# Strassen's products in the last two token tiles of a sparse-attention and feed-forward kernel

## The chip, the cores and the metric

The kernel runs on one core of one Trainium2 chip. The metric is the device time of one execution in microseconds (us), and the figure of a kernel is the median over its executions. The engines are TensorE (PE; its weight loads are PEld), VectorE (DVE), ScalarE (ACT), GpSimd (POOL) and SyncE (SP, which issues the transfers).

## The reference

Eight batches with eight heads of 576 tokens and 64 elements pass through a sparse causal attention: four heads see a local window of 32 tokens, four see every 32nd token. The result, 4608 tokens by 512, goes through a feed-forward layer without a nonlinearity other than a product.

```python
scores = scale * np.matmul(q, k.transpose(0, 1, 3, 2))      # masked, softmax
x = attn_out.transpose(0, 2, 1, 3).reshape(B * S, H * D)    # 4608 x 512
a = x @ w1                                                  # w1, w2: 512 x 1024
b = x @ w2
h = a * b @ w3                                              # w3: 1024 x 1024
return h @ w_out                                            # 1024 x 512
```

## The kernel before

The attention output is kept transposed in fp16, in four tiles `xT[0]` to `xT[3]` of 128 features by 4608 tokens. `xT[hp]` holds head pair `hp`; pairs 0 and 1 are the local heads, 2 and 3 the strided ones. `w3 @ w_out` is formed once on the chip into `w34`, so that the feed-forward layer is three matmuls for each tile of 512 tokens: there are nine such tiles (0 to 8).

For a tile and a block `jc` of 128 of the 1024 d_ff columns, `a` (L956) sums four matmuls of 128x512 into one PSUM bank, one for each `xT`. ACT copies it to SBUF (`asb`, L309). `b` (L972) sums four more into another bank, and DVE multiplies both into `abt` in fp16 (L978, "mul"). After eight blocks four output groups `o` of 128 tokens follow (L992), eight matmuls each. ACT copies each to `osb` and SP stores it. The groups are written as `o6_2` for tile 6, group 2, and `a7_0` for tile 7, block 0.

The attention of batch b runs between the matmuls of tile b-1. For each head pair it has a score group on PE (`S7_3` is batch 7, pair 3; L794), an exponential on ACT (L811), a mask on DVE (L818), a value group on PE in two halves (`X7_3_0` and `X7_3_1`) and a normalisation. For pairs 2 and 3 that is `ln` and `rcp` on ACT (L874, L885) for each half and then two multiplications on DVE into `xT` (L901), called "norm" here. Pairs 0 and 1 are normalised on DVE and transposed back by PE. Pair 3 of a batch is last.

PSUM has four single banks (kind "f": `a`, `b`, `o`, transposes) and two pairs (kind "B": scores and values). Inputs are loaded as fp32 into eight staging tiles `st0` to `st7` of 128x1024 and cast by POOL.

Every piece of work is an `Op` with engine, estimated duration, dependencies, buffers taken and given back, and a rank. `Plan.order` (L89) walks through time and gives each free engine the ready operation with the lowest rank. The result is one fixed order for each engine; at run time each engine works through its order and waits at semaphores. The ranks of tile t lie at 100 + 24 t, and those of the attention come from `_arank`:

```python
base = {0: 40, 1: 60}.get(b, 100 + 24 * (b - 1) - 4)
a = plan.op(f"a{t}_{jc}", {"PE": 864}, fa, ..., rank=100 + 24 * t + 2 * jc + 1)
h = plan.op(f"o{t}_{ts}_{pt}_{hf}", ..., rank=100 + 24 * t + 17 + 2 * ts + 0.001 * hf)
```

Of the kernel before, what the change touches and what calls it, by code (L numbers as in the profile page):

```python
# [16 lines left out]


def _arank(b, i, ph):
    base = {0: 40, 1: 60}.get(b, 100 + 24 * (b - 1) - 4)  # L20
    span = {0: 4, 1: 12}.get(b, 24)
    return base + span * (i / 4 + OFF[ph])


def _loads():
# [6 lines left out]
    for b in range(2, 8):  # L32
# [6 lines left out]

CFG = dict(loads=_loads(), arank=_arank, frank=lambda j: 50 + j, slack=100,  # L40
           pord=lambda b: (2, 3, 0, 1) if b < 2 else (0, 1, 2, 3), tsplit=False, dmaf=1.08, nhr=8, cast=dict(w1=dict(POOL=1040)),
           first=('DVE', 'ACT', 'POOL'), early=0, pm=4, nx=4, nstg=8, new=(2, 3), lb=3, ll=4, nat={'POOL': 1160})


def _ap(t: bass.AP, off_add, dims):
# [215 lines left out]
def kernel(  # L261
# [12 lines left out]
    cfg = CFG  # L274
# [24 lines left out]
    NSTG = cfg.get("nstg", 8)  # L299
    NABT = cfg.get("nabt", 3)  # L300
    stgs = [consts.tile([P, DF], FP32, name=f"st{i}") for i in range(NSTG)]
    plan = Plan(dict(f=NF, B=2, stg=NSTG, asb=2, osb=3, rcp=2, xqs=2, xqd=cfg.get("nxq", 2), w3n=3, abt=NABT))

    def pin(ins):
        return tc.keep_in_program_order(ins)
# [383 lines left out]
    for b in range(B):  # L689
# [30 lines left out]
        for pi, hp in enumerate(cfg["pord"](b)):  # L720
# [78 lines left out]
            for g in range(2):  # L799
# [31 lines left out]
                                                 ptms[pslot][0:kr, h * 288 + i * w:h * 288 + (i + 1) * w],  # L831
                                                 start=True, stop=True))

                def fpo(e, b=b, hp=hp, g=g, pk=pk, w=w, m=m, kr=kr, local=local, pslot=pslot):
                    xps = bank("B", pk, [P, 2, 512], FP32)
                    vt = (v16L if local else v16S)[b % 2]
                    for i in range(m):
                        for h in range(2):
                            c0 = h * 288 + i * w
                            pin(nc.tensor.matmul(xps[0:w, h, i * 65:(i + 1) * 65], ptms[pslot][0:kr, c0:c0 + w],  # L840
                                                 vt[0:kr, 2 * (hp % 2) + h, g * m + i, 0:D + 1],
                                                 start=True, stop=True))

                if old:
                    fp = fpo
                pv = PVop[(b, hp, g)] = plan.op(pk, {"PE": 246}, fp, deps=[mo, onesop[(b % 2, local)]] + vop[(b, hp, g)],
                                                take=[("B", pk)], rank=rank(f"P{g}"), soft=True)
                ptmu[pslot] = pv
                newPV[g] = pv

                if old:
                    def fn(e, pk=pk, w=w, m=m, g=g, xk=xk):
                        xps = bank("B", pk)
                        rcp = att.tile([P, 2, 4], FP32, tag="rcq", name="rcq")
                        if not xk:
                            xqs = att.tile([P, 4, 2, D], FP16, tag="xqs", bufs=2, name="xqs")
                            live[("xqs", pk)] = xqs
                        elif g == 0:
                            live[xk] = att.tile([LQ, LT, 2, D], FP16, tag="xqd", bufs=cfg.get("nxq", 2), name="xqd")
                        if xk:  # L860
                            xqs = live[xk][:, g * m:g * m + m]
                        xv = xps[0:w, :, 0:m * 65].rearrange("p h (i e) -> p h i e", e=65)
                        pin(nc.vector.reciprocal(out=rcp[0:w, :, 0:m], in_=xv[:, :, :, D]))
                        pin(nc.vector.tensor_mul(xqs[0:w, 0:m].rearrange("p i h d -> p h i d"), xv[:, :, :, 0:D],  # L864
                                                 _ap(rcp, 0, [[rcp.ap[0][0], w], [4, 2], [1, m], [0, D]])))

                    norms.append(plan.op(f"norm{nm2}_{g}", {"DVE": 190 + 60 + (554 if local else 690)}, fn,
                                         deps=[pv] + norms, take=[] if xk and g else [xk or ("xqs", pk)], give=[("B", pk)], rank=1))
                    continue


# [65 lines left out]
                                     deps=[t2, wf], give=[("f", tk)], rank=1)]  # L937


    for t in range(NTILE):  # L940
        tok = bass.ds(t * NT, NT)
        bs = range(t * NT // S, (t * NT + NT - 1) // S + 1)
        xd = [x for b in bs for h in range(4) for x in xTop[(b, h)]]
        muls = []

        def fz(e, t=t):
            big[("abt", t)] = ffn.tile([P, KF, NT], FP16, tag="abt", bufs=NABT, name="abt")

        z = plan.op(f"abt{t}", {"PE": 0}, fz, deps=xd, take=[("abt", f"abt{t}")], rank=100 + 24 * t - 20)
        for jc in range(KF):  # L950
            js = bass.ds(jc * P, P)

            def fa(e, jc=jc, t=t, js=js, tok=tok):
                ps = bank("f", f"a{t}_{jc}", [P, NT], FP32)
                for ci in range(KM):
                    pin(nc.tensor.matmul(ps, w1h[:, ci, js], xT[ci][:, tok], start=(ci == 0), stop=(ci == KM - 1)))  # L956

            a = plan.op(f"a{t}_{jc}", {"PE": 864}, fa, deps=[z] + w1c[jc], take=[("f", f"a{t}_{jc}")],
                        rank=100 + 24 * t + 2 * jc + 1)

            def fs(e, jc=jc, t=t):
                asb = ffn.tile([P, NT], FP32, tag="asb", bufs=2, name="asb")
                live[("asb", t, jc)] = asb
                copy(e, asb, bank("f", f"a{t}_{jc}"))

            s = plan.op(f"asb{t}_{jc}", cfg.get("asb", {"ACT": 590}), fs, deps=[a], take=[("asb", f"{t}_{jc}")],
                        give=[("f", f"a{t}_{jc}")], rank=4)

            def fb(e, jc=jc, t=t, js=js, tok=tok):
                ps = bank("f", f"b{t}_{jc}", [P, NT], FP32)  # L970
                for ci in range(KM):
                    pin(nc.tensor.matmul(ps, w2h[:, ci, js], xT[ci][:, tok], start=(ci == 0), stop=(ci == KM - 1)))  # L972

            bb = plan.op(f"b{t}_{jc}", {"PE": 864}, fb, deps=xd + w2c[jc] + [a], take=[("f", f"b{t}_{jc}")],
                         rank=100 + 24 * t + 2 * jc + 1.001)

            def fu(e, jc=jc, t=t):
                pin(nc.vector.tensor_mul(big[("abt", t)][:, jc, :], bank("f", f"b{t}_{jc}"), live[("asb", t, jc)]))  # L978

            muls.append(plan.op(f"mul{t}_{jc}", {"DVE": 690}, fu, deps=[bb, s],  # L980
                                give=[("f", f"b{t}_{jc}"), ("asb", f"{t}_{jc}")], rank=4))
        for ts in range(NT // P):
            last = t == NTILE - 1 and ts == NT // P - 1
            parts = ((0, 256), (256, 128), (384, 128)) if last else ((0, DM),)
            for pt, (n0, nw) in enumerate(parts):
                key = f"o{t}_{ts}_{pt}"
                h = None
                for hf in range(2):
                    def fo(e, t=t, ts=ts, hf=hf, key=key, n0=n0, nw=nw):
                        ps = bank("f", key, [P, nw], FP32) if hf == 0 else bank("f", key)  # L990
                        for ci in range(4 * hf, 4 * hf + 4):
                            pin(nc.tensor.matmul(ps, big[("abt", t)][:, ci, bass.ds(ts * P, P)],  # L992
                                                 w34[:, ci, bass.ds(n0, nw)], start=(ci == 0),
                                                 stop=(ci == KF - 1)))

                    h = plan.op(f"o{t}_{ts}_{pt}_{hf}", {"PE": 864 * nw // DM}, fo,
                                deps=[muls[4 * hf + i] for i in range(4)] + w34op[8 * hf:8 * hf + 8] + [h],
                                take=[("f", key)] if hf == 0 else [], rank=100 + 24 * t + 17 + 2 * ts + 0.001 * hf,
                                give=[("abt", f"abt{t}")] if ts == 3 and hf == 1 and pt == len(parts) - 1 else [])

                ok = "asb" if pt else "osb"

                def fc(e, key=key, nw=nw, ok=ok):
                    osb = ffn.tile([P, nw], FP32, tag=ok, bufs=3 if ok == "osb" else 2, name="osb")
                    live[("osb", key)] = osb
                    copy(e, osb, bank("f", key))

                oe = {"ACT": 170 + 4 * nw // 5, "DVE": 70 + 6 * nw // 5} if last else cfg.get("osb", {"ACT": 590})
                c = plan.op(f"osb{key}", oe, fc, deps=[h], take=[(ok, key)], give=[("f", key)], rank=4)

                def fd(e, key=key, t=t, ts=ts, n0=n0, nw=nw):
                    eng = nc.scalar if e == "ACT" else nc.sync
                    pin(eng.dma_start(out_r[t * (NT // P) + ts][:, bass.ds(n0, nw)], live[("osb", key)]))

                plan.op(f"st{key}", cfg.get("st", {"SP": 450}), fd, deps=[c],
                        give=[(ok, key)], rank=4.5, dma=750 * nw // DM, store=True)
# [42 lines left out]
```

## Time and profile before

| what | before |
|---|---|
| median of 13 runs | 272.5 us (271.52 to 274.1) |
| the profiled execution, its span | 271.57 us, 269.8 us |
| PE busy, matmuls | 259.4 us (96%), 2265 |
| DVE busy, ACT busy, POOL busy | 168.9 us, 156.1 us, 146.4 us |
| bytes moved by transfers | 54.41 MB, 202 GB/s |
| granted TensorE clock | 0.997 |

The page comes from one execution. Busy time is given as a share of the span; PE's is modelled, since matmuls overlap in the array, and a matmul of 512 columns is listed with 379 ns although the next one starts about 216 ns later. The 40 slices show when an engine works, and the chain of waits shows which work was last in line before the end. A group's idle time is that of its engine just before it, with the work that ended it.

### The profile page before, as it was taken

What the parts mean: (1) busy time and instruction counts of PE and PEld (TensorE: products, weight loads), DVE (VectorE), ACT (ScalarE), POOL (GpSimd) and SP (SyncE); (2) the same over time, 40 slices, a digit from 0 to 9 for tenths busy, and PEclk for the clock granted to TensorE, in tenths of its full rate; (3) what the DMA queues carried; (4) which work ended last, traced back from release to release, by engine and by line L of the source; (5) the groups of instructions that cost most, each with busy time, mean ns of one, the idle gap of its engine ahead of it and who ended that gap; (6) DMA issues with size and microseconds to landing.
All of it is one profiled execution on the core that took longest, in us unless ns stands there. A gap on an engine that the chain in (4) does not pass through costs nothing.

```text
span 269.8 us, 6083 instructions
## 1 busy us (share of the span) xinstructions
PE 259.4 (96%) x2265; PEld 141.5 (52%) x2265; DVE 168.9 (63%) x324; ACT 156.1 (58%) x280; POOL 146.4 (54%) x172
## 2 busy tenths in 40 slices
PE   7887899999999999999999999999999999999994
PEld 2466786545565545544544555455545554444443
DVE  6645566885787758766884787487659762422321
ACT  2870467764677764775577647756764774333331
POOL 6676997689879447964793389626980000000000
PEclk9999999999999999999999999999999999999998
DMA  7999999999699899899989998999995013003004
GB/s 242 348 359 272 348 356 351 307 272 315 210 258 231 147 269 206 192 202 278 209 203 188 266 165 201 177 278 197 191 206 146 0 41 117 2 22 135 0 4 155
DMA packets 72766, 54.41 MB, mean 202 GB/s; under 512 B 44256, under 2 KB 62048, under 8 KB 72736
## 3 DMA queue, kind: packets, MB, share of 16 engines
q1 hardware_dynamic: 72736, 54.02, 82.4%
q8 instruction: 18, 0.29, 0.5%
q14 instruction: 12, 0.10, 0.1%
HBM read 38.93 MB, written 9.44 MB: 179 GB/s over the span
## 4 chain that ended last, share of the span: by engine, by line
PE 87%; DMA 7%; SPq 2%; POOL 1%; issue 1%; DVE 1%; ACT 0%; POOLq 0%
PE ps_o L992 23%; PE ps_b L972 23%; PE ps_a L956 23%; DMA st<-in_moe_w_dram 7%; PE ps_S L794 4%; PE ps_mm L669 3%; PE ps_X L840 3%; PE ps_X L830 3%; PE ps_U L921 2%; SPq L316 2%; PE ps_T L747 1%; POOL w3n L313 1%; PE ps_tr L649 1%; PE ps_S L784 0%; PE ps_R L695 0%
## 5 line engine op out<-in xcount | busy, mean ns | idle before, releaser
L972 PE MATMUL ps_b<-xT,w2h 128*128 128x512 f16 x288 | 73.8, 379 | 0.2 <-DVE kTL L311 0.2
L956 PE MATMUL ps_a<-xT,w1h 128*128 128x512 f16 x288 | 73.9, 379 | 0.0
L978 DVE TENSOR_TENSOR abt<-ps_b,asb 128x512 f16<-128x512 f32 x72 | 49.7, 690 | 38.3 <-PE ps_b L972 35.1
L309 ACT COPY asb<-ps_a 128x512 f32<-128x512 f32 x72 | 42.1, 587 | 49.2 <-PE ps_a L956 48.9
L992 PE MATMUL ps_o<-w,abt 128*128 128x512 f16 (+2 forms) x304 | 67.3, 368 | 0.0
L313 POOL CAST xs<-st 80x1024 f16<-80x1024 f32 (+1 forms) x36 | 33.2, 941 | 19.3 <-DMA st<-in_q_dram 17.0
L972 PEld LDWEIGHTS <-w2h 128*128 128x128 f16 x288 | 26.7, 98 | 28.6 <-POOL w2h L313 0.7
L992 PEld LDWEIGHTS <-abt 128*128 128x128 f16 x304 | 27.2, 98 | 27.5
L956 PEld LDWEIGHTS <-w1h 128*128 128x128 f16 x288 | 26.5, 98 | 27.5
L811 ACT ACTIVATE ps_S<-ps_S 128x576 f32<-128x576 f32 (+2 forms) x56 | 32.8, 627 | 12.1 <-PE ps_S L794 12.1
L309 ACT COPY osb<-ps_o 128x512 f32<-128x512 f32 (+1 forms) x36 | 20.8, 578 | 24.1 <-PE ps_o L992 21.0
L901 DVE TENSOR_TENSOR xT<-ps_X,rcp 64x288 f16<-64x288 f32 x56 | 25.2, 450 | 13.6 <-ACT rcp L885 12.8
L313 POOL CAST v16L<-st 32x768 f16<-32x768 f32 (+1 forms) x32 | 26.3, 821 | 6.5 <-DMA st<-in_v_dram 4.9
L818 DVE TENSOR_TENSOR ptm<-ps_S,maskL 128x576 f16<-128x576 f32 x28 | 19.8, 750 | 9.4 <-ACT ps_S L811 9.3
L864 DVE TENSOR_TENSOR xqs<-ps_X,rcq 96x384 f16<-96x384 f32 (+1 forms) x36 | 20.5, 568 | 1.2
L313 POOL CAST v16S<-st 72x1024 f16<-72x1024 f32 (+1 forms) x16 | 16.5, 1037 | 5.6 <-DMA st<-in_v_dram 5.6
L885 ACT ACTIVATE rcp<-ps_X 64x576 f32<-64x576 f32 x28 | 18.1, 647 | 0.9
L874 ACT ACTIVATE ps_X<-ps_X 64x576 f32<-64x576 f32 x28 | 17.7, 631 | 0.3
L669 PE MATMUL ps_mm<-woh,xT 128*128 128x256 f16 x128 | 16.0, 273 | 1.6 <-POOL woh L313 1.6
L840 PEld LDWEIGHTS <-ptm 128*96 128x96 f16 (+1 forms) x224 | 14.5, 123 | 5.5 <-issue 0.2
L313 POOL CAST x<-st 128x1024 f16<-128x1024 f32 x14 | 14.4, 1039 | 4.7 <-DMA st<-in_q_dram 2.7
L311 DVE COPY xT<-ps_U 128x576 f16<-128x576 f16 x18 | 8.8, 490 | 11.3 <-PE ps_U L921 11.3
(82 smaller groups left out, 265.7 us busy)
## 6 DMA issues: line engine op xcount, KB each, us to landing
out_dram<-osb SPq DMA_DIRECT2D x35, 256.0 KB
st<-in_moe_w_dram SPq DMA_DIRECT2D x16, 512.0 KB
st<-in_v_dram SPq DMA_DIRECT2D x16, 288.0 KB
st<-in_v_dram SPq DMA_DIRECT2D x16, 256.0 KB
st<-in_q_dram SPq DMA_DIRECT2D x7, 512.0 KB
st<-in_k_dram SPq DMA_DIRECT2D x7, 512.0 KB
st<-in_q_dram SPq DMA_DIRECT2D x10, 256.0 KB
st<-in_k_dram SPq DMA_DIRECT2D x10, 256.0 KB
```

Of the source, the lines that this page charges most:

```text
L309: pin(nc.scalar.copy(out=out, in_=in_))
L313: pin(nc.gpsimd.tensor_copy(out=out, in_=in_))
L669: pin(nc.tensor.matmul(ps, w3T(kc)[:, js], big["woh"][:, kc, ns], start=(kc == 0), stop=(kc == KF - 1)))
L811: pin(nc.scalar.activation(out=sps, in_=sps, func=AF.Exp, bias=0.0, scale=scale))
L818: pin(nc.vector.tensor_mul(ptm[0:kr, 0:576].rearrange("p (h a x) -> p h a x", h=2, x=w), pte[0:kr].rearrange("p h (a x) -> p h a x", x=w), ...
L840: pin(nc.tensor.matmul(xps[0:w, h, i * 65:(i + 1) * 65], ptms[pslot][0:kr, c0:c0 + w], vt[0:kr, 2 * (hp % 2) + h, g * m + i, 0:D + 1], sta ...
L864: pin(nc.vector.tensor_mul(xqs[0:w, 0:m].rearrange("p i h d -> p h i d"), xv[:, :, :, 0:D], _ap(rcp, 0, [[rcp.ap[0][0], w], [4, 2], [1, m] ...
L901: pin(nc.vector.tensor_mul(o, i0, i1))
L956: pin(nc.tensor.matmul(ps, w1h[:, ci, js], xT[ci][:, tok], start=(ci == 0), stop=(ci == KM - 1)))
L972: pin(nc.tensor.matmul(ps, w2h[:, ci, js], xT[ci][:, tok], start=(ci == 0), stop=(ci == KM - 1)))
L978: pin(nc.vector.tensor_mul(big[("abt", t)][:, jc, :], bank("f", f"b{t}_{jc}"), live[("asb", t, jc)]))
L992: pin(nc.tensor.matmul(ps, big[("abt", t)][:, ci, bass.ds(ts * P, P)], w34[:, ci, bass.ds(n0, nw)], start=(ci == 0), stop=(ci == KF - 1)))
```

## The change

Tiles 7 and 8 are treated together for the d_ff blocks 2 to 7. Split the 512 features into two halves and take tile 7 and tile 8 as the two halves of the rows: X11, X12 are tile 7's halves and X21, X22 are tile 8's. The weights are W11, W12 (first half of `w1`, `w2`) and W21, W22. The four wanted blocks (`a` and `b` of both tiles) are then a 2 by 2 block product. It is computed with seven products P1 to P7 of two matmuls each (Winograd's form of Strassen's algorithm) in place of eight. Blocks 0 and 1 keep the old form in both tiles.

- Weight sums T1 to T4, each 128 x 2 x 1024 fp16, go to four staging tiles. Their first halves (columns 0 to 511) are made on DVE, the second halves on POOL behind a small copy called `gate`.
- Input sums S1 to S4, each two pieces (c = 0, 1) of 128x512 fp16, go to two staging tiles. With S1 = X21 + X22, S2 = S1 - X11, S3 = X11 - X21 and S4 = X12 - S2, piece c = 1 of S1, S2 and S4 is made on DVE (430 in the plan) and the other five on POOL (1150). Piece c = 1 of S1 adds `xT[1]` and `xT[3]`.
- In each block the bank A takes P1, then P6, P7 and P4 on top of it. A pair of banks B = (E, G) takes P2 on E, and P5 and then P3 on G. ACT copies A after P1 (`e`), G after P5 (`p5`), A after P6 (`u2`) and, from the third block on, E after P2 (`c11`). DVE adds `u2` to G in PSUM (`u4`), forms `c22` = A + `p5`, and multiplies twice into `abt` (`h1`, `h2`); in blocks 2 and 3 it also adds E to `c11`.
- The output groups of tiles 7 and 8 come after all of these blocks. The attention of batches 2 to 7 is ranked 2 later.

```diff
-    base = {0: 40, 1: 60}.get(b, 100 + 24 * (b - 1) - 4)
+    base = {0: 40, 1: 60}.get(b, 100 + 24 * (b - 1) - 2)
...
+           sf=(2, 3, 4, 5, 6, 7), te={'DVE': 690}, nr=(1, 25, 2, 0), te1='POOL', se=((3, 0), (3, 1), (1, 0), (2, 0), (4, 0)))
...
+        for i, x, y in ((1, (1, 2), (1, 1)), (3, (2, 2), (1, 2)), (2, (2, 2), 1), (4, (2, 1), 2)):
+            for hf in range(2):
...
+                    pin(eng.tensor_sub(Tt[i][:, :, cs], W[x][:, :, cs], b0[:, :, cs]))
...
+        for i in (3, 1, 2, 4):
+            for c in range(2):
...
+                    if i == 3:
+                        a0, a1, op = xT[c][:, tk1], xT[c][:, tk2], eng.tensor_sub
+                    elif i == 1:
+                        a0, a1, op = xT[c][:, tk2], xT[2 + c][:, tk2], eng.tensor_add
+                    elif i == 2:
+                        a0, a1, op = sv(1), xT[c][:, tk1], eng.tensor_sub
+                    else:
+                        a0, a1, op = xT[2 + c][:, tk1], sv(2), eng.tensor_sub
+                    pin(op(sv(i), a0, a1))
...
+            gate = plan.op("gate", {"POOL": 200}, lambda e: pin(
+                nc.gpsimd.tensor_copy(out=scr, in_=St[1][:, 1, 1, 0:2])), deps=[Sx[(4, 1)], T[(4, 0)]], rank=11)
...
+        prods = dict(P1=(A[1], lambda: W[(1, 1)], "A", xd(0, b1) + xd(1, b1)),
+                     P5=(SL(1), lambda: Tt[1], "G", sd(1) + [T[(1, hf)]]),
+                     P6=(SL(2), lambda: Tt[2], "A", sd(2) + [T[(2, hf)]]),
+                     P2=(A[2], lambda: W[(2, 1)], "E", xd(2, b1) + xd(3, b1)),
+                     P7=(SL(3), lambda: Tt[3], "A", sd(3) + [T[(3, hf)]]),
+                     P4=(A[4], lambda: Tt[4], "A", xd(2, b2) + xd(3, b2) + [T[(4, hf)]]),
+                     P3=(SL(4), lambda: W[(2, 2)], "G", sd(4)))
...
+                for c in range(2):
+                    pin(nc.tensor.matmul(bk(x), rt()[:, c, js], lf(c), start=st_ and c == 0,
+                                         stop=c == 1, skip_group_check=not st_))
...
+        q1 = prod("P1", take=[kA], rank=R, extra=list(zs.values()))
+        q5 = prod("P5", take=[kB], rank=R + .1, extra=[q1])
...
-                                take=[("f", key)] if hf == 0 else [], rank=100 + 24 * t + 17 + 2 * ts + 0.001 * hf,
+                                take=[("f", key)] if hf == 0 else [], rank=100 + 24 * t + 17 + 2 * ts + 0.001 * hf + (16 if SF and t >= tA else 0),
```

## The prediction

> **What bounds the kernel now.** I read the busy times first, then the slices, the chain of waits, the costliest groups, and last the timeline around the edit.
>
> ```profile
> PE 259.4 (96%) x2265; PEld 141.5 (52%) x2265; DVE 168.9 (63%) x324; ACT 156.1 (58%) x280; POOL 146.4 (54%) x172
> ...
> PE   7887899999999999999999999999999999999994
> ...
> POOL 6676997689879447964793389626980000000000
> PEclk9999999999999999999999999999999999999998
> ...
> PE 87%; DMA 7%; SPq 2%; POOL 1%; issue 1%; DVE 1%; ACT 0%; POOLq 0%
> ...
> L978 DVE TENSOR_TENSOR abt<-ps_b,asb 128x512 f16<-128x512 f32 x72 | 49.7, 690 | 38.3 <-PE ps_b L972 35.1
> L309 ACT COPY asb<-ps_a 128x512 f32<-128x512 f32 x72 | 42.1, 587 | 49.2 <-PE ps_a L956 48.9
> ```
>
> PE is at 9 tenths from slice 6 on, it is 87% of the chain, and the other engines idle because they wait for it (38.3 us before L978, 49.2 us before the copies). In the second half PE never waits, so a removed matmul is worth its full pitch, and any new wait of PE is lost in full. The chain lists `a` and `b` as four matmuls in 0.86 us: 0.216 us each.
>
> What decides this case is the slack where attention ends and tile 7 begins. The timeline there, in order of time:
>
> ```profile
> 216.60 0.43 PE L794 MATMUL ps_S<-qT,kTS 64*128 64x72 f16 x16
> 216.94 1.16 ACT L811 ACTIVATE ps_S<-ps_S 72x576 f32<-72x576 f32 x2 [0.52 <-PE ps_S L794]
> ...
> 219.51 0.63 ACT L874 ACTIVATE ps_X<-ps_X 64x576 f32<-64x576 f32 x1
> 219.83 0.42 PE L830 MATMUL ps_X<-ptm,v16S 72*128 72x72 f16 x8
> 220.09 4.49 PE L992 MATMUL ps_o<-w,abt 128*128 128x512 f16 x20
> ...
> 221.39 0.65 ACT L885 ACTIVATE rcp<-ps_X 64x576 f32<-64x576 f32 x1
> ...
> 222.07 0.92 DVE L901 TENSOR_TENSOR xT<-ps_X,rcp 64x288 f16<-64x288 f32 x2 [0.30 <-ACT rcp L885]
> ...
> 224.41 1.03 PE L956 MATMUL ps_a<-xT,w1h 128*128 128x512 f16 x4
> ```
>
> `S7_3` starts at 216.60 and the last norm ends at 222.07 + 0.92 = 222.99, 6.4 us later. `a7_0` (224.41) reads `xT[3]` with its fourth matmul only, at about 225.06. That is 2.1 us of slack, bought by the 20 `o6` matmuls (220.09) behind `X7_3_1` (219.83).
>
> [...] Here PE waited 1.64 us once (at 20 us) and the clock stayed at 1.00; in the last window, where PE is done for 3.7 us, it reads 0.91.
>
> **The change part by part.**
>
> *Matmuls.* A block of both tiles costs 16 matmuls before and 14 after; six blocks save 12. The built program agrees: 2253 matmuls for 2265, with the same 23 warm-up ones. Gain 12 x 0.216 = **2.59 us**, if PE stays as dense.
>
> *The boundary.* In the new order PE does: `o6_2`, `S7_3`, `o6_3` (8 matmuls), P1 of block 2, `X7_3_0`, P1 of block 3, `X7_3_1`, P1 of blocks 4 and 5, P5 of block 2. So `S7_3` has moved behind three of the four `o6` groups, and only P1s stand behind `X7_3_1`. P5 needs S1; its second matmul needs piece 1, which DVE makes after the last norm. ACT's new order is: copy of `o6_2`, two exponentials, copy of `o6_3`, `c11` copy of block 2, `ln`, `rcp`, `ln`, `rcp`. With the durations above, time 0 where `S7_3` starts, 0.2 us from PE to ACT (`a7_0`'s last matmul issues until 225.28, its copy starts at 225.48):
>
> - PE: `S7_3` to 0.37, `o6_3` to 2.10 (8 x 0.216), P1 to 2.53, `X7_3_0` (0.26) to 2.79, P1 to 3.22, `X7_3_1` to 3.48, two P1 to 4.34, first matmul of P5 to 4.55.
> - ACT: copy 0.20 to 0.79, exponentials (1.16) to 1.95, `o6_3` copy 2.30 to 2.89, `c11` to 3.48, then the four `ln`/`rcp` (219.51 to 222.04, 2.53) to 6.01.
> [...]
>
> The stall is 7.47 - 4.55 = **2.92 us**. Below: were `osb` and `c11` not in ACT's way, the four `ln`/`rcp` still could not start before 2.99, 0.49 earlier, so at least 2.4 us. [...]
>
> *Behind the stall* DVE is the late engine: S2 and S4 to 8.39, `c11` (after P2) 9.18 to 9.87, then in its order and 0.69 each `u4`, `c22`, `u4` of block 3, `h1`, `h2`, `c11` and `c22` of block 3, the last one ending at 14.70. PE waits for `c22` (P4 at 11.31, idle 0.14), for the second `u4` (P3 at 12.00, 0.26), for `h1` which frees the bank of the next P5 (0.26), for `h2` which frees that of `a7_0` (0.26), for the second `c22` (0.09), and 0.04 for `u2`: together **1.05 us**. From there the sixteen matmuls of old form for blocks 0 and 1 of each tile are spread between the products, and a block asks 4 x 0.69 = 2.76 us of DVE and 4 x 0.587 = 2.35 us of ACT against 14 x 0.216 = 3.02 us of PE; I find no further wait. In-place adds from PSUM to PSUM on DVE have no row; I take L978's 0.69. At 0.59 they give back some 0.3 us, at 0.85 they cost about 1 us. ACT's copies within PSUM go by L811 (633 ns for 576 elements), which is the 587 of 512.
>
> [...]
>
> *Moved.* Attention 2 ranks later in batches 2 to 7. At tile 5 to 6, `o5_2`, `o5_3`, `S7_0` and three matmuls follow `X6_3_1` (4.5 us), and the norm ends some 2.9 us after it: 1.6 us are left, cost 0. SP issues the same transfers; its eight last stores now come every 1.73 us, as the last four did, and the transfer share was 0.31 in the last window: cost 0.
>
> *Sum* on the profiled run: 271.57 - 2.59 + 2.92 + 1.05 = 272.95, that is +1.4 us. That run lies 0.93 under the median of 272.5, so 272.5 + 1.4 = **273.9**.
>
> **The rivals.**
>
> - *The boundary stall is no more than the saving.* Place: second matmul of the first P5. For it: only one wait is certain, and idle DVE and ACT time elsewhere (slices 30 to 40 show 2 to 4 tenths) may absorb the later ones. With 2.4 us and no later wait the sum is -0.2, 272.3; a gain of over 0.3% needs stalls under 1.77 us. Against: the ACT chain alone makes 2.4. It decides from where `ln` of `X7_3_0` starts 1.15 us earlier than I have it.
> [...]
> [...]
> - *The change works in full*: no wait, -2.6, 269.9. Against: the orders above.
>
> **How the numbers follow.** A difference under 0.3% (0.8 us) can't be told from none. Forecast 0.52 (nearly all of it slower, 0.05 within 0.3%), stall equal to the saving 0.18 (0.15 within, 0.03 faster), clock 0.14, late sum 0.12, in full 0.04. So faster 0.07, same 0.20, slower 0.73. The range leaves out the full gain below and the worst of the two late cases above: 272.2 to 276.0.
>
> **What would show it.** Right: PE with 2253 matmuls, a wait of PE of nearly 3 us that ends at DVE's input sum, near the end of attention, and short ones by DVE in the next 8 us; DVE's input sum at 0.42 and weight sum at 0.69 us. Wrong: PE dense behind `X7_3_1`, a clock below 1.00 in the stretch after it, a PE wait ended by POOL, or a weight sum that holds masks and makes PE wait inside tile 6.

## The result and the profile after

The changed kernel takes 275.5 us (median of 11 runs, 274.25 to 278.48) against 272.5 for the kernel before (48 runs). The ratio is 1.0117, interval 1.0093 to 1.0142: by the ratio about 3.2 us slower. The sign is the forecast one. The size is more than twice the forecast 1.4 us, though the median lies inside the range of 272.2 to 276.0.

The first profiled execution (278.48 us, span 276.6) is the longest of its kernel, over 1.5% above the fastest one, and counts as a slow run that the ratio leaves out. Its first `a` starts 2 us later than in before, although up to there the orders of the engines are the same. A second profile of the same kernel took 273.58 us (label e8 below). The main readings use that one, and stages are compared from the start of the first `a` matmul to that of the last `o` matmul, which leaves out the start and the last stores:

| profile | first `a` | last `o` | between, us | to before |
|---|---|---|---|---|
| before | 43.8 | 265.8 | 222.0 | |
| after, first profile | 45.8 | 272.4 | 226.7 | +4.7 |
| after, second profile (e8) | 43.8 | 267.3 | 223.6 | +1.6 |
| e1, ranks put back | 44.9 | 265.3 | 220.4 | -1.6 |
| e2, useless matmuls | 44.6 | 268.2 | 223.6 | +1.6 |
| e3, five output buffers | 44.7 | 269.6 | 224.9 | +2.9 |
| e4, later ranks alone | 43.4 | 265.2 | 221.8 | -0.2 |
| e5, weight sums on POOL | 44.3 | 264.5 | 220.2 | -1.8 |
| e6, e2 and e3 together | 43.8 | 267.3 | 223.5 | +1.5 |
| e7, seven blocks | 44.8 | 264.8 | 220.0 | -2.0 |
| e9, six blocks, `o6` as filler | 43.6 | 264.7 | 221.1 | -0.9 |

The page of the first profile, against the lines shown of before:

```profile
PE 261.3 (94%) x2253; PEld 142.0 (51%) x2253; DVE 180.2 (65%) x343; ACT 161.7 (58%) x292; POOL 161.6 (58%) x182
...
PE   7878799999999999999999999999979996999994
...
PEclk9979999999999999999999999999999998999999
```

Twelve matmuls are gone (2253). PE has two dents where before had none: a 7 in slice 30, in tile 6, and a 6 in slice 34, at the end of attention. In slice 34 the clock row shows an 8 (the 7 in its slice 3 lies ahead of the first `a`).

The timeline of PE in the second profile, where attention ends (start, length, the last column idle time before and what ended it):

```profile
221.50 0.43 PE L795 MATMUL ps_S<-qT,kTS 64*128 64x72 f16 x16
221.86 1.90 PE L1155 MATMUL ps_o<-w,abt 128*128 128x512 f16 x8
223.60 0.59 PE L1053 MATMUL ps_Aw<-xT,w1h 128*128 128x512 f16 x2
224.03 0.42 PE L831 MATMUL ps_X<-ptm,v16S 72*128 72x72 f16 x8
224.29 0.60 PE L1053 MATMUL ps_Aw<-xT,w1h 128*128 128x512 f16 x2
224.73 0.42 PE L831 MATMUL ps_X<-ptm,v16S 72*128 72x72 f16 x8
224.99 1.03 PE L1053 MATMUL ps_Aw<-xT,w1h 128*128 128x512 f16 x4
227.48 0.38 PE L1053 MATMUL ps_Bw<-st,st 128*128 128x512 f16 x1 [1.46 <-ACT rcp L888]
228.98 0.81 PE L1053 MATMUL ps_Bw<-st,st 128*128 128x512 f16 x3 [1.12 <-DVE st L990]
```

`S7_3` starts at 221.50 and the second matmul of P5 (the first of the last line) at 228.98, 7.48 us later. The forecast had 7.47. DVE's S1 piece (L990) ends the wait, as forecast. Between the end of the four P1 matmuls, 224.99 + 4 x 0.216 = 225.85, and 228.98 PE issued one matmul, so 2.9 us are lost.

DVE of the first profile there: the norm of `X7_3_1`, and then the three S pieces at the forecast 0.42 us:

```profile
231.13 0.92 DVE L904 TENSOR_TENSOR xT<-ps_X,rcp 64x288 f16<-64x288 f32 x2 [0.30 <-ACT rcp L888]
232.14 0.42 DVE L990 TENSOR_TENSOR st<-xT,xT 128x512 f16<-128x512 f16 x1
232.60 0.42 DVE L990 TENSOR_TENSOR st<-st,xT 128x512 f16<-128x512 f16 x1
233.06 0.42 DVE L990 TENSOR_TENSOR st<-xT,st 128x512 f16<-128x512 f16 x1
```

### The profile page after: what moved, and what is told of

The parts are those of the page before. It is cut to its first block, busy times and chain, and to the rows that moved or that the text cites. A ratio compares the mean times of both kernels' runs of the same rounds, so it can differ in the third digit from the quotient of the medians.

```text
span 276.6 us, 6088 instructions
## 1 busy us (share of the span) xinstructions
PE 261.3 (94%) x2253; PEld 142.0 (51%) x2253; DVE 180.2 (65%) x343; ACT 161.7 (58%) x292; POOL 161.6 (58%) x182
## 5 line engine op out<-in xcount | busy, mean ns | idle before, releaser
L1135 PE MATMUL ps_b<-xT,w2h 128*128 128x512 f16 x240 | 61.5, 379 | 1.7 <-ACT osb L310 1.5
L1119 PE MATMUL ps_a<-xT,w1h 128*128 128x512 f16 x240 | 61.6, 379 | 0.0
L310 ACT COPY asb<-ps_a 128x512 f32<-128x512 f32 x60 | 35.1, 589 | 31.5 <-PE ps_a L1119 30.6
L1141 DVE TENSOR_TENSOR abt<-ps_b,asb 128x512 f16<-128x512 f32 x60 | 41.3, 688 | 10.4 <-PE ps_b L1135 7.1
L904 DVE TENSOR_TENSOR xT<-ps_X,rcp 64x288 f16<-64x288 f32 x56 | 25.2, 450 | 18.5 <-ACT rcp L888 18.0
L1135 PEld LDWEIGHTS <-w2h 128*128 128x128 f16 x240 | 22.4, 98 | 26.2 <-issue 2.4
L1119 PEld LDWEIGHTS <-w1h 128*128 128x128 f16 x240 | 21.1, 98 | 20.1 <-issue 0.3
L819 DVE TENSOR_TENSOR ptm<-ps_S,maskK 72x576 f16<-72x576 f32 x20 | 14.1, 747 | 4.4 <-ACT ps_S L812 4.4
```

The lines of the kernel that those rows point to most:

```text
L310: pin(nc.scalar.copy(out=out, in_=in_))
L819: pin(nc.vector.tensor_mul(ptm[0:kr, 0:576].rearrange("p (h a x) -> p h a x", h=2, x=w), pte[0:kr].rearrange("p h (a x) -> p h a x", x=w), ...
L904: pin(nc.vector.tensor_mul(o, i0, i1))
```

## The experiments

**The theories.** Boundary: PE waits for S1 at the end of attention because `S7_3` stands behind three `o6` groups, with little behind `X7_3_1`. Clock: the idle time there lets the TensorE clock fall. Store: ACT's copy of `o5_3` waits for a store and holds a bank that PE needs in tile 6. Rivals: the products are too dear for ACT and DVE, or later attention alone is the loss.

**e1, the ranks put back.**

```diff
-    base = {0: 40, 1: 60}.get(b, 100 + 24 * (b - 1) - 2)
+    base = {0: 40, 1: 60}.get(b, 100 + 24 * (b - 1) - 4)
```

> The changed kernel with the attention ranks put back (4 in place of 2 subtracted); nothing else is edited, but the planner then puts S7_3 behind the first half of o6_0 and all of o6_2, o6_3, a7_0 to b7_1 and a8_0 behind X7_3_1. Boundary theory (the loss is PE waiting for S1 at the end of attention, not the cost of the products): the wait of nearly 3 us is gone and the short waits behind it too, so 272.5 - 2.6 + 0.5 = about 270.4, a ratio to before of 0.992. Rival, products too dear (seven products with their copies and adds cannot be kept dense): slower than before as the changed kernel was, 1.008 to 1.012, with PE waits inside the stretch of the products.

Measured 271.57 us, ratio 0.9956 (0.9929 to 0.9983). The same products at the same prices are now faster than before, so the rival of dear products falls. The gain is 1.2 us, not 2.1. PE in the new place:

```profile
221.66 0.42 PE L831 MATMUL ps_X<-ptm,v16S 72*128 72x72 f16 x8
221.92 3.62 PE L1155 MATMUL ps_o<-w,abt 128*128 128x512 f16 x16
225.38 1.03 PE L1119 MATMUL ps_a<-xT,w1h 128*128 128x512 f16 x4
...
229.69 1.03 PE L1053 MATMUL ps_Aw<-xT,w1h 128*128 128x512 f16 x4
230.56 1.03 PE L1053 MATMUL ps_Bw<-st,st 128*128 128x512 f16 x4
...
236.74 0.59 PE L1053 MATMUL ps_Aw<-xT,w1h 128*128 128x512 f16 x2
237.56 0.59 PE L1053 MATMUL ps_Aw<-st,st 128*128 128x512 f16 x2 [0.23 <-ACT ps_Bw L310]
238.18 0.59 PE L1053 MATMUL ps_Bw<-xT,w1h 128*128 128x512 f16 x2
```

P5 comes 8.6 us after `X7_3_1` and waits for nothing. What is left are short waits on ACT's and DVE's copies. A pair of matmuls should take 0.43 us; from 236.74 to 237.56 it is 0.82. Such excesses add up to 1.1 us, and -2.6 + 1.1 = -1.5 fits the -1.6 in the table.

**e2, useless matmuls in the wait.**

```diff
                 if nm == "P1":
                     bank(*kA, [P, NT], FP32)
+                    for _ in range(7 if n_ == 3 else 0):
+                        pin(nc.tensor.matmul(bk("A"), w34[:, 0, 0:P], w34[:, 0, :], start=True, stop=True))
```

> The changed kernel with seven matmuls of no use (into the bank of block 5, just ahead of its P1, 1.5 us), so that PE works in the first half of its wait; the order is otherwise the same. Clock theory (the idle wait lets the TensorE clock fall to half for some 2 us behind it, which cost 1.6 us in the profiled run): clock 1.00 at 232 to 236 us and 1.0 to 1.6 us off the changed kernel, a ratio to before of 1.006 to 1.008. Boundary theory without the clock: nothing gained, 1.012, since P5 starts when S1 is there in any case.

Measured 274.47 us, ratio 1.0067 (1.0045 to 1.0088). Seven more matmuls make the kernel 1.4 us faster than the changed one at 1.0117. The intervals of the two ratios don't overlap. The clock is 1.00 in every window from 226 to 236 us of its profile; that alone would show little, since e8 below has 1.00 there as well. The boundary alone can't explain the gain: the second matmul of P5 still starts 7.48 us after `S7_3` (229.80 and 222.32).

**e3, five output buffers.**

```diff
-                    osb = ffn.tile([P, nw], FP32, tag=ok, bufs=3 if ok == "osb" else 2, name="osb")
+                    osb = ffn.tile([P, nw], FP32, tag=ok, bufs=5 if ok == "osb" else 2, name="osb")
```

> The changed kernel with five output buffers osb in place of three; the order is the same. Store theory (ACT's copy of o5_3 waits for the store of o5_0, which stands behind transposes on SP, and holds a bank that b6_1 of PE needs, 1.5 us in the profiled run): that wait is gone and 0.5 to 1.5 us are won, a ratio of 1.006 to 1.010. Rival: the wait was peculiar to that one execution, ratio 1.012 as before.

Measured 275.41 us, ratio 1.0089 (1.0059 to 1.0119). In its profile tile 6 has no wait, but the interval reaches 1.0117: a gain by the buffers isn't shown, and e8 and e2 have no wait there with three buffers either. This execution shows the clock fall. By windows (PE, PEld, DVE, ACT and POOL busy, then granted clock, DMA share, GB/s):

```profile
226.00:228.00 2.00, 0.93 (x6) 0.19 (x3) 0.84 (x2) 1.94 (x4) 0.00 (x0) 1.00 0.35 131
228.00:230.00 2.00, 0.53 (x2) 0.23 (x3) 1.56 (x5) 0.92 (x2) 0.00 (x0) 0.83 0.00 0
230.00:232.00 2.00, 2.00 (x6) 0.67 (x5) 0.68 (x2) 1.17 (x2) 1.22 (x2) 0.50 0.00 0
232.00:234.00 2.00, 2.00 (x9) 0.83 (x8) 0.87 (x2) 1.17 (x2) 2.00 (x2) 0.82 0.00 0
234.00:236.00 2.00, 1.99 (x10) 0.61 (x8) 2.00 (x4) 0.00 (x0) 2.00 (x2) 1.00 0.00 0
```

PE counts as fully busy at 230 to 232, but issues 6 matmuls where 9 would fit. The nine from P5's second one (229.85) to 233.20 take 3.35 us; in e8, with the clock at 1.00, the same nine take 228.98 to 230.92, 1.94 us. The fall costs 1.4 us here, and e3 lies 1.3 us above e8 in the table.

**e4, the later ranks alone**, in the kernel before.

```diff
-    base = {0: 40, 1: 60}.get(b, 100 + 24 * (b - 1) - 4)
+    base = {0: 40, 1: 60}.get(b, 100 + 24 * (b - 1) - 2)
```

> The kernel before with 2 in place of 4 subtracted from the attention ranks, no Strassen products. Boundary theory: 0, since o6_2, o6_3 and three matmuls of a7_0 (4.1 us) still stand behind X7_3_1 and no P5 waits for S1; ratio 0.999 to 1.001. Store theory: up to 1.5 us in tile 6, 1.000 to 1.005. Rival, the later attention alone is the loss: 1.011.

Measured 272.22 us, ratio 0.9989 (0.9971 to 1.0007). Later attention alone costs nothing.

**e5, first weight sums on POOL**, ranks as in the change. Of the long line of settings, the part that differs:

```diff
-te={'DVE': 690}
+te={'POOL': 2400}
```

> The changed kernel, attention 2 ranks later as it has it, with the first halves of the weight sums on POOL in place of DVE. The planner then places S7_3 behind the first half of o6_0 and has o6_2, o6_3, a7_0 to b7_1 and a8_0 behind X7_3_1. Boundary theory (neither the later ranks nor the DVE sums alone do it, but the two together push S7_3 behind o6_2): PE no longer waits for S1, ratio 0.993 to 0.997 like the experiment with the ranks put back. Rival, the later ranks alone: 1.007 to 1.012. Second rival, sums on POOL come late behind its casts: a PE wait that ends at a POOL weight sum, 1.000 to 1.005.

Measured 270.70 us, ratio 0.9948 (0.9930 to 0.9966). The ranks of the change stand, and the wait is gone. So neither the later ranks (e4) nor the DVE sums with the old ranks (e1) make the loss. Both together do: only then does the planned order of PE put `S7_3` behind `o6_2`. In e1 and in e5, 28 of the 32 `o6` matmuls follow `S7_3`; in the changed kernel 8 do. That the estimates of the DVE sums and the ranks push the scores back in the plan is read from these orders.

**e6, e2 and e3 together.**

> The changed kernel with both the seven matmuls of no use ahead of P1 of block 5 and five output buffers; same order. If clock and store wait are the two terms that the forecast had at zero, what is left is the forecast's own sum, -2.6 + 2.9 + 1.05 = +1.4 us: ratio 1.004 to 1.006. If another loss is hidden, 1.008 or more.

Measured 273.62 us, ratio 1.0054 (1.0031 to 1.0076), which is +1.5 us. That is close to the forecast's own sum of +1.4 us.

**e7, seven blocks, meant to be fast.** The ranks of e1, the POOL sums of e5, the buffers of e3, and, in parts of longer lines (`nr` ranks the blocks that keep the old form):

```diff
-sf=(2, 3, 4, 5, 6, 7)
-nr=(1, 25, 2, 0)
+sf=(1, 2, 3, 4, 5, 6, 7)
+nr=(1, 13, 2, 0)
...
-+ (16 if SF and t >= tA else 0),
++ (16 if SF and t >= tA else 0) + (30 if t == 6 and ts > 2 else 0),
```

> A version meant to be fast: ranks put back to 4, first halves of the weight sums on POOL, the products for seven blocks (1 to 7) in place of six, o6_3 ranked 30 later so that it fills gaps behind the end of attention, five output buffers. 14 matmuls less are 3.0 us; with no wait of over 0.1 us in the stretch of the products the ratio to before is 0.989 to 0.991. If DVE and ACT cannot keep up with seven blocks, short waits return and it is 0.993 to 0.997.

Measured 270.18 us, ratio 0.9928 (0.9903 to 0.9953): faster than before and than the change, by less than hoped. Three places in its stretch of products lose 0.46, 0.40 and 0.34 us. Of 3.0 us saved 1.8 are left; the table has 2.0.

**e8, the changed kernel again.**

> The changed kernel once more, unedited, on the chip of this call, for a second profile and more executions beside the experiments. Boundary, clock and store theories: P5 of block 2 again waits in two parts, together 2.9 us, in every execution; the clock falls to half behind it (0.5 in the two microseconds after the wait); the 1.5 us wait in tile 6 may be absent, as it was in the run with the useless matmuls. Ratio 1.009 to 1.013; 1.004 to 1.006 if the clock happens not to fall in these executions.

Measured 275.20 us, ratio 1.0116 (1.0079 to 1.0153). Its profile is the second one above: the boundary wait of 2.9 us, no wait in tile 6, and no fall of the clock behind the wait:

```profile
226.00:228.00 2.00, 0.40 (x2) 0.13 (x2) 1.39 (x4) 1.94 (x4) 0.00 (x0) 1.00 0.01 2
228.00:230.00 2.00, 1.02 (x5) 0.48 (x5) 1.69 (x4) 0.68 (x3) 0.09 (x1) 1.00 0.00 0
230.00:232.00 2.00, 2.00 (x11) 0.88 (x9) 1.15 (x2) 1.54 (x3) 2.00 (x2) 1.00 0.00 0
```

This execution took 273.58 us, 0.3 from the forecast 273.9; it is the fastest of the kernel's 18. With the same wait the clock falls in some executions only, and the expected 0.5 is missing in this one.

**e9, six blocks with `o6_2` and `o6_3` as filler**: e1 and e5 together, three buffers, and

```diff
-+ (16 if SF and t >= tA else 0),
++ (16 if SF and t >= tA else 0) + (30 if t == 6 and ts > 1 else 0),
```

> Like the seven-block version, but with six blocks, o6_2 and o6_3 both ranked 30 later, and three output buffers: ranks put back to 4, first halves of the weight sums on POOL. 12 matmuls less are 2.6 us; the planner leaves no wait of over 0.1 us in the stretch of the products. If the short waits of the seven-block run (0.7 us) come from the seventh block's load on ACT and DVE, they are gone here and the ratio is about 0.991; if from the order alone, 0.994 to 0.996.

Measured 271.72 us, ratio 0.9984 (0.9966 to 1.0002). Both expectations miss. Its PE timeline has five places with 0.46, 0.40, 0.34, 0.33 and 0.33 us too much, together 1.9 of the 2.6 saved. Two of them are before `P2`s:

```profile
224.47 0.59 PE L1053 MATMUL ps_Aw<-st,st 128*128 128x512 f16 x2
225.36 0.59 PE L1053 MATMUL ps_Bw<-xT,w1h 128*128 128x512 f16 x2 [0.30 <-ACT p L310]
...
230.11 0.59 PE L1053 MATMUL ps_Aw<-st,st 128*128 128x512 f16 x2
230.94 0.59 PE L1053 MATMUL ps_Bw<-xT,w1h 128*128 128x512 f16 x2 [0.24 <-ACT p L310]
```

By the releaser, P2 writes the pair of banks from which ACT is copying `p5` (read from the trace, not tested apart). The code gives P2 no such dependency: it asks for P5 in the first two blocks and for `e` in the others. The planner therefore takes P2 as ready early, and PE stands until the copy is done. More filler at the boundary doesn't help there, and the waits don't come from a seventh block.

## Why the prediction was wrong in size

**Right.** Twelve matmuls at 0.216 us. The boundary: 7.48 us from `S7_3` to P5's second matmul against 7.47, a loss of 2.9 us. The 7.47, and the 8.39 for S2 and S4, use 0.42 us for a DVE piece of the input sums, which no run of before shows; in the first profile its three pieces took 0.42 us each. POOL's halves of the weight sums took 2.12 to 2.13 us (first profile and e5). Behind the first 60 us no PE wait ends at POOL, so no run shows the late sum, to which the forecast gave 0.12. The step "the boundary" had one detail wrong: P5's first matmul waits too. It needs a pair of banks, and the normalisation of `X7_3_0` frees it late (in the first profile and e3 DVE's `xT`, L904, ends this wait). The sum stays, since the second matmul ends last. e6 measured the whole sum: +1.5 for +1.4.

**Right in part by luck: the short waits.** They were put at 1.05 us. In e8 the starts of PE's matmuls give 1.46: 0.72 in the places of the forecast, and two waits where it found no further one, 0.41 at P2 of block 4 and 0.33 at 247.93. The 0.72 is smaller than forecast because DVE's operations follow each other every 0.60 us, though each is listed with 0.69, the step that the forecast took (its own estimate for a step of 0.59, some 0.3 us given back, fits). From the first profile:

```profile
238.45 0.68 DVE L1088 TENSOR_TENSOR abt<-ps_Bw,c 128x512 f16<-128x512 f32 x1
239.05 0.68 DVE L1091 TENSOR_TENSOR abt<-ps_Aw,c 128x512 f16<-128x512 f32 x1
239.65 0.68 DVE L1080 TENSOR_TENSOR c<-ps_Bw,c 128x512 f32<-128x512 f32 x1
```

The DVE weight sums, at 0.69 us in the forecast, a price that no run of before shows, took 0.68 to 0.69 us where POOL did nothing beside them. In the changed kernel, e2, e3 and e6 the first two of the four were longer, together by 1.0 to 1.6 us; no PE wait followed.

**Wrong: the clock was left out of the sum.** It stood at 0.14 among the chances. Its price was 1.6 us in the first profile, 1.4 in e3 and 1.4 by e2's ratio, so the sum put at nothing a term of 1.4 us. A wait of 1.64 us behind which the clock stayed at 1.00, as in before, says nothing of a wait of 2.9 us. Stretches of 3.41 us, first those ahead of and in the fall of the first profile, then the same of e3 (columns as in e3 above):

```profile
229.08:232.49 3.41, 0.95 (x4) 0.20 (x3) 2.15 (x5) 2.54 (x5) 0.00 (x0) 1.00 0.16 61
232.49:235.91 3.42, 3.29 (x8) 1.13 (x8) 0.98 (x4) 1.76 (x3) 2.37 (x3) 0.50 0.00 0
...
225.91:229.32 3.41, 1.40 (x10) 0.41 (x7) 1.80 (x4) 2.94 (x5) 0.00 (x0) 1.00 0.20 77
229.32:232.73 3.41, 2.88 (x7) 1.02 (x7) 1.28 (x3) 1.72 (x3) 1.95 (x2) 0.50 0.00 0
```

The clock stood at 0.50 for the whole of a stretch of 3.41 us, and PE had been busy for 0.95 and 1.40 us (41%) of the stretch before, not idle throughout. In e8 PE was busy for only about 0.8 us of the 3.41 us ahead of P5's second matmul (228.98; estimate from its timeline: 225.57 to 226.02, and 0.38 us from 227.48), and the clock stayed at 1.00. So neither the wait of 2.9 us nor PE's busy time ahead of its end tells whether the clock falls; what decides it is not shown. The first profile has one more stretch at 0.50, from 17.45 to 20.87, as long as the other.

The profile of before held a sign that the clock can fall so soon, in the windows behind PE's last matmul, which ends at 266.05:

```profile
267.50:268.00 0.50, 0.00 (x0) 0.00 (x0) 0.00 (x0) 0.00 (x0) 0.00 (x0) 1.00 0.48 138
268.00:268.50 0.50, 0.00 (x0) 0.00 (x0) 0.00 (x0) 0.00 (x0) 0.00 (x0) 0.63 0.41 117
268.50:269.00 0.50, 0.00 (x0) 0.00 (x0) 0.00 (x0) 0.00 (x0) 0.00 (x0) 0.50 0.00 0
```

The clock fell between 268.0 and 268.5, some 2 us after PE had stopped, which is less than the wait of 2.9 us.

How often it falls can be read from the mean clock of each execution: one fall takes 3.41 x 0.5 us of some 272, which makes 0.994. The mean is 0.994 or less in 21 of the 30 executions of the changed kernel and e3, in 7 of the 34 of e2 and e6, which fill the wait, and in 16 of the 119 of before beside these experiments. Falls ahead of the first `a`, as in the first profile at 17.45, are in all of these counts. If they are as frequent in each, the wait brings a fall in about 0.6 of the executions (estimate: (21/30 - 7/34) / (1 - 7/34)), against 0.14 in the forecast.

**Open: "SP issues the same transfers ... cost 0".** The first profile has this in tile 6:

```profile
204.99 0.59 ACT L310 COPY osb<-ps_o 128x512 f32<-128x512 f32 x1 [2.43 <-DMA out_dram<-osb]
...
205.62 1.02 PE L1135 MATMUL ps_b<-xT,w2h 128*128 128x512 f16 x4 [1.47 <-ACT osb L310]
```

The copy of `o5_3` waits for the store of `o5_0` to give its buffer back, and `b6_1` waits for the bank of `o5_3`. The forecast looked at SP's work and not at who waits for a landing. Before had a wait of 1.4 us at the same copy, and no PE wait followed. How many executions have it is not settled: it is absent in e8 and e2, and the gains by five buffers (1.0089 against 1.0117, and 1.0054 against 1.0067) are within the intervals. The last stores are a second open term: from the start of the last `o` to the end of the span before takes 4.0 us, the profiles with six blocks 4.1 to 4.7.

Together: 1.6 us by the forecast's terms (e8) and 1.4 by the clock (e2 against the changed kernel, with an error of about 0.9 by the two intervals). The 0.2 left of 3.2 are within the error, so neither store is shown to cost anything.

## What to carry to other kernels

Where one engine is never idle, a saving is judged by what stands behind the last producer of the stage before: count the work that the new order leaves there against the chain that it must cover. Here 1 us of covering work stood against about 4 us. Price a long wait of TensorE at more than its length: behind the 2.9 us here the clock fell in some executions, at 1.4 us (e3) and 1.6 us (first profile) more. When two harmless edits shift the same chain, test each alone before blaming either.

## What the runs showed of the hardware

- Behind an idle time of 2.6 us with a single matmul in it the granted clock was 0.50 for 3.41 us in some executions, at a cost of 1.4 us (e3) and 1.6 us (first profile) of PE time; in the profiles of e2 and e6, behind a wait of 1.15 and of 1.2 us, it stayed at 1.00.
- In five profiles (both of the changed kernel, e2, e3, e6) the first two DVE weight sums, beside POOL's copy and casts, took 0.69 to 1.40 and 1.52 to 1.65 us, the other two 0.68. In the first profile POOL's copy took 1.43 us in place of 1.15. In e1, with POOL idle beside them, all four took 0.68 to 0.69.
- DVE's in-place add from PSUM to PSUM took 0.69 to 0.70 us for 128x512, and ACT's copy within PSUM 0.57 to 0.61, as much as the same operations into SBUF (0.69 and 0.59).
